# Pooled attention and a gated feed-forward on one core: next batch's loads, the order of the transpose queue, and when GpSimd pools

## The chip, the cores and the metric

One of the eight cores of a Trainium2 chip runs the kernel. The metric is the device time of one execution in microseconds (us), lower is better.

## The reference

Attention over pooled keys and values, then a feed-forward with the activation h * cos(h). Sizes: 8 batches, 8 heads, 576 rows, head size 64; keys and values are averaged over groups of 8 rows, which leaves 72. The feed-forward takes 4608 tokens of width 512 through 2048 and back.

```python
k_p = k.reshape(B, H, Sp, 8, D).mean(axis=3); v_p = the same of v
attn = softmax(q @ k_p.T / sqrt(D))
x = (attn @ v_p).transpose(0, 2, 1, 3).reshape(4608, 512)
h = x @ w_in
out = (h * cos(h)) @ w_out
```

## The kernel before

**Tiles.** The tokens are cut into nine tiles of 512 (loop `t`, line 550), the attention into eight batches of 576 rows. While tile t goes through the feed-forward, the attention of batch b = t + 1 is done between its matmuls, and the keys and values of batch b + 1 = t + 2 are loaded and pooled. The first batches and tile 0 have a path of their own; the change bears on tiles 1 to 7.

**Up phase** of a tile. Eight pairs of chunks of 128 columns (`up_mm`, line 336): TensorE multiplies w_in by xT into PSUM, ScalarE takes the cosine (line 352), VectorE multiplies both into `g_sb` (line 356). From tile 1 on, the output product is a fast scheme with seven smaller products instead of eight, for which VectorE forms the sums g1 to g4 of quarters of `g_sb` (`put_g`, line 381, both operands bf16 in SBUF). In steady tiles the first halves of g1 and g2 are formed after the fourth pair, of g3 after the fifth, of g4 after the sixth (line 570).

**Down phase.** The seven products (line 420) alternate between two banks, A and Bb; after each, VectorE reads the bank (`each`, lines 434 and 436; the `reads` list). In between TensorE does the attention of batch b: scores (line 222), whose exponentials ScalarE takes (line 229), and `values_rows` (line 276) for three chunks of 128 rows, later a fourth. `values_rows` ends with two VectorE operations (lines 287 and 289) that leave `x_rows`, and a DMA transpose on the sync queue that writes xT (line 293). The next tile's up phase needs xT.

**What sets the order.** There is no scheduler (`manual_schedule`): each engine and each queue runs in the order of the text. Three queues matter here.

- The sync queue (SP): four xT transposes of a tile, then its eight stores of 128 KB each (`rows_out`, line 451), issued in the last two reads (lines 446 and 447); then, in the next tile's up phase, the transpose of q (line 195, after the first pair) and of the pooled k (line 182, after the third), for the next batch.
- GpSimd: at the end of a tile's text a copy of one element of `kk` into `gate` (line 688). It makes GpSimd wait until the transpose of the pooled k has landed. Then GpSimd issues the loads of k, q and v of batch b + 1 (lines 114, 95, 114), and pools k and v in `pool_add` (lines 145 to 159): four steps from the staged tile into `half_sums` (line 151), two in `half_sums` (line 153), then two that write `kp2` for k, or one that writes `vz` for v. All are additions of 72 x 512 elements.
- VectorE: `g_sb` products, g sums, bank reads and the two operations of `values_rows`, in the order of the text.

The loads cast from fp32 to bf16 and move 576 KB each into SBUF. `kv_st` has two buffers, `qT` two, `o_two` two.

Of the kernel before, what the change touches and what calls it, by code (L numbers as in the profile page):

```python
# [12 lines left out]
ADD = mybir.AluOpType.add  # L13
# [7 lines left out]
def kernel(  # L21
# [9 lines left out]
    nc = tc.nc  # L31
    B, H, S, D = q.shape
# [37 lines left out]
    HF, HT, HM = FFCH // 2, TILE // 2, d_model // 2  # L70
    g1, g2, g3, g4 = [wpool.tile([128, HF, HT], BF16, name=f"g{i}") for i in range(1, 5)]
# [4 lines left out]
    kk = [wpool.tile([128, H, SpA], BF16, name=f"kk{i}") for i in range(2)]  # L76
# [9 lines left out]

    staged = {}

    def even_view(src, b, j0=0, j1=KCH):
        return src[b, 2 * j0:2 * j1].rearrange("(j a) (p t) d -> (a p) j (t d)", a=2, t=ROW)
# [18 lines left out]
    def load_kv(b, which, src):  # L111

        st = kv_tile()[:Sp, 0:H * POOL * D].rearrange("p (h t d) -> p h t d", h=H, t=POOL)
        nc.gpsimd.dma_start(out=st.rearrange("p h t d -> p h (t d)"),
                            in_=src[b].rearrange("h (p t) d -> p h (t d)", t=POOL))
        staged[which, b] = st

    def load_q(b):
        q_tile(b)
        load_even(staged["q", b], b, q)  # L120
# [21 lines left out]
            for r in range(2):  # L142
                copy(out=dst[half[r], pj0:pj1, a, 0:Sp], in_=ps[half[a]])

    def pool_add(b, which):

        st = staged.pop((which, b))
        x, s = st, half_sums
        add = nc.gpsimd.tensor_tensor
        for h in range(0, H, 2):  # L150
            add(out=s[:, h:h + 2], in0=x[:, h:h + 2, 0:4, :], in1=x[:, h:h + 2, 4:8, :], op=ADD)  # L151
        for h in range(0, H, 4):
            add(out=s[:, h:h + 4, 0:2, :], in0=s[:, h:h + 4, 0:2, :], in1=s[:, h:h + 4, 2:4, :], op=ADD)  # L153
        if which == "k":
            for slot in range(2):
                add(out=kp2[b % 2][:Sp, :, slot, :], in0=s[:, :, 0, :], in1=s[:, :, 1, :], op=ADD)  # L156
        else:
            s = s.rearrange("p (j a) t d -> p j a t d", a=2)
            add(out=v_part(b), in0=s[..., 0, :], in1=s[..., 1, :], op=ADD)
# [21 lines left out]
    def k_transpose(b):  # L181
        nc.sync.dma_start_transpose(out=kk[b % 2], in_=kp2[b % 2].rearrange("p h s d -> p (h s d)"))
# [198 lines left out]
    def put_g(k, i):  # L381
        f0, f1 = 4 * i, 4 * i + 4
        t1f1, t1f2, t2f1, t2f2 = [g_part(f, t, f0, f1) for t in range(2) for f in range(2)]
        out, x, y, op = {1: (g1, t2f1, t2f2, ADD), 2: (g2, g1[:, f0:f1], t1f1, SUB), 3: (g3, t1f1, t2f1, SUB),
                         4: (g4, t1f2, g2[:, f0:f1], SUB)}[k]
        nc.vector.tensor_tensor(out=out[:, f0:f1], in0=x, in1=y, op=op)  # L386
# [5 lines left out]
    def down_products(t):  # L392

        def of(w, m=0):
            return lambda fc: w[fc // 4][:, fc % 4, m * HM:(m + 1) * HM]

        def part(x):
            return lambda fc, p: x[:, fc, p * 128:(p + 1) * 128]

        apart = t == NT - 1  # L400
        if apart:
            A, Bb = [[x[:, 0:HM] for x in two] for two in (obanks, (banks[1][:, 0, :], banks[2][:, 0, :]))]
        else:
            A, Bb = [[obanks[i][:, p * HM:(p + 1) * HM] for p in range(2)] for i in (1, 0)]
        products = [
            (A, True, part(g_part(0, 0, 0, HF)), of(w_out_sb[0:2])),
            (Bb, True, part(g_part(1, 0, 0, HF)), of(w_out_sb[2:4])),
            (A, True, part(g2), of(w2)),
            (Bb, True, part(g1), of(w1)),
            (A, False, part(g3), of(w3)),  # L410
            (Bb, False, part(g4), of(w_out_sb[2:4], 1)),
            (A, False, part(g_part(1, 1, 0, HF)), of(w4)),
        ]
        mms = []
        for n, (bank, first, g, w) in enumerate(products):
            order = [(fc, p) for fc in range(HF) for p in range(2)]
            if apart and n == 6:
                order.sort(key=lambda x: x[1])
            for fc, p in order:
                mms.append(lambda bank=bank, first=first, g=g, w=w, fc=fc, p=p: nc.tensor.matmul(  # L420
                    bank[p], lhsT=g(fc, p), rhs=w(fc),
                    start=(first and fc == 0 and (apart or p == 0)), stop=(fc == HF - 1 and (apart or p == 1)),
                    skip_group_check=not first))

        p1, v16, q15 = [msb.tile([128, 2, HM], FP32, name=n, tag=n, bufs=1) for n in ("p1_sb", "v_sb", "q_sb")]
        o1, o2 = [msb.tile([128, 2, d_model], FP32, name="o_two", tag="o_two", bufs=2) for _ in range(2)]
        m1, m2 = slice(0, HM), slice(HM, d_model)

        def each(out, bank, other=None, m=slice(0, HM), tk=None):

            for p in range(2) if apart else (slice(0, 2),):
                ps = bank[p] if apart else obanks[1 if bank is A else 0].rearrange("p (a m) -> p a m", a=2)
                if other is None:
                    (nc.scalar.copy if t >= B - 1 else nc.vector.tensor_copy)(out=out[:, p, m], in_=ps)  # L434
                else:
                    nc.vector.tensor_tensor(out=out[:, p, m], in0=ps, in1=other[:, p], op=ADD)  # L436
                if apart and tk is not None:
                    rows_out(t, tk, out, (p,), m, (nc.sync, nc.scalar))

        reads = [  # L440
            lambda: each(p1, A),
            lambda: each(o1, Bb, p1, m1, 0),
            lambda: each(v16, A, p1),
            lambda: each(q15, Bb, p1),
            lambda: each(o2, A, q15, m2, 1),
            lambda: (each(o1, Bb, v16, m2, 0), apart or rows_out(t, 0, o1)),
            lambda: (each(o2, A, p1, m1, 1), apart or rows_out(t, 1, o2)),
        ]
        return [mms[i * 2 * HF:(i + 1) * 2 * HF] for i in range(7)], reads

    def rows_out(t, tk, o, ps=(0, 1), m=slice(0, d_model), queues=(nc.sync, nc.sync)):
        rows_of = out.rearrange("(b p t) m -> b t p m", b=B, t=ROW)
        for p in ps:
            for i, rows in enumerate(half):
                b_, pos = divmod((t * TILE + tk * HT + p * 128) // 64 + i, ROW)
                queues[i].dma_start(out=rows_of[b_, ORDER[pos], :, m], in_=o[rows, p, m])
# [36 lines left out]
    gate = consts.tile([1, 1], BF16, name="gate")  # L493
# [56 lines left out]
    for t in range(NT):  # L550
# [5 lines left out]
        for n, fp in enumerate(up_order(t)):  # L556
            up_mm(t, fp, 2 if n < 2 else 0)
            between = ()
            if t == 0:
                if fp == 4:  # L560
                    puts = pool_k_mm(1, obanks[0], 0, 2), pool_k_mm(1, obanks[1], 2, 4)
                elif fp in (5, 6):
                    g0 = 9 * (fp - 5)
                    puts = q_transpose_mm(1, obanks[0], g0, g0 + 5), q_transpose_mm(1, obanks[1], g0 + 5, g0 + 9)
                if fp in (4, 5, 6):
                    puts[0](vec)
                    between = ((puts[1], act),)
            up_g(t, fp, between)
            if 0 < t and 3 <= n < 6:
                put_gs(*[(k, 0) for k in (((3,), (1,), ()) if t == 1 else ((1, 2), (3,), (4,)))[n - 3]])  # L570
            if 0 < t and b < B:
                if n == 0:
                    q_transpose(b)
                elif n == 2:
                    k_transpose(b)
        mms = [(ms, fc) for ms in range(4) for fc in range(FFCH)]
        if t == 0:
            mms = [(ms, fc) for hm in range(2) for cg in (0, 2, 1, 3) for ms in range(2 * hm, 2 * hm + 2)
# [36 lines left out]
        else:  # L615
# [17 lines left out]
            def muls():  # L633
                while later:
                    later.pop(0)()
# [12 lines left out]
                put_g(2, 0)  # L648
            put_gs((1, 1), (2, 1))
            reads[0]()  # L650
            put_g(3, 1)
            reads[1]()
            if t == 1:
                put_g(4, 0)
            if steady:
                values_rows(*u0)
            product(2)
            reads[2]()
            muls()
            if steady:  # L660
                values_rows(*u1)
                values_rows(*u2)
# [20 lines left out]
            reads[6]()  # L683
        if t < B:
            sin_tables()
        if 0 < t and b + 1 < B:

            nc.gpsimd.tensor_copy(out=gate, in_=kk[b % 2][0:1, 0, 0:1])
        if b + 1 < B:
            load_kv(b + 1, "k", k)  # L690
            load_q(b + 1)
            load_kv(b + 1, "v", v)
            if t == 0:
                put_weights(0, nc.gpsimd, (3, 2, 4))
                put_weights(1, nc.gpsimd, (1,))
            pool_add(b + 1, "k")
            pool_add(b + 1, "v")
# [1 line left out]
_INS = ['q', 'k', 'v', 'moe_w_in', 'moe_w_out']  # L699
_OUTS = [((4608, 512), 'float32')]  # L700
# [25 lines left out]
```

The softmax here doesn't subtract the row's maximum and nothing guards it: scores larger than these inputs give would overflow.

## Time and profile before

| | us |
|---|---|
| median of 3 runs | 291.74 |
| lowest, highest | 290.35, 293.71 |
| span of the profiled run | 288.6 |
| first up matmul of tiles 2, 3, 4, 5, 6, 7, 8 | 84.09, 113.20, 143.89, 173.15, 202.56, 231.93, 258.57 |
| one step of pooling, line 151 / 153 / 156 (mean) | 1.195 / 1.305 / 1.329 |
| product into `g_sb`, line 356 (mean) | 1.221 |
| sum of two quarters of `g_sb`, line 386 (mean) | 0.760 |
| xT transpose, issue to landing (median, longest) | 5.8, 9.6 |
| load of k / q / v, issue to landing (median) | 7.7 / 10.2 / 14.4 |

How to read it: PE is TensorE, PEld its weight loads, DVE VectorE, ACT ScalarE, POOL GpSimd, SPq the sync queue. In a timeline each line has start, length, engine, line of the kernel, operation, output and input with their shapes, and in brackets how long the engine was idle just before and what ended that. A length includes time in which the operation stood at the head of its engine and could not go on.

### The profile page before, as it was taken

The numbers are of one execution on the slowest core, as the hardware profiler recorded it, in microseconds if no ns is written. First come the engines' busy times: TensorE is split into PE (matmuls) and PEld (weight loads), VectorE is DVE, ScalarE is ACT, GpSimd is POOL, SyncE is SP. The second block draws the span as 40 slices with busy tenths as digits, with TensorE's granted clock in tenths as the row PEclk, the third lists the DMA queues.
The fourth block names the chain that finished last, engine by engine and source line by source line (L and its number), as shares of the span: only waits on it lengthen the run. The fifth ranks groups of instructions, "written<-read, shape, count | busy, mean of one in ns | idle before, by whom it ended". The sixth has DMA issues, their size and how long they took to land.

```text
span 288.6 us, 5827 instructions
## 1 busy us (share of the span) xinstructions
PE 275.1 (95%) x2338; PEld 175.9 (61%) x2360; DVE 217.5 (75%) x314; ACT 164.2 (57%) x193; POOL 149.7 (52%) x145
## 2 busy tenths in 40 slices
PE   7889999999979999999799999999999999999994
PEld 2545554447854696468645884488448854884583
DVE  6458747799947995799549966996699669856972
ACT  3786798368147735773556655665557456436600
POOL 8563079996698359933995299529930000000000
PEclk9999999999999999999999999999999999999999
DMA  7999999554998699769977998699680243006014
GB/s 161 200 207 206 206 205 216 120 99 53 184 119 172 89 179 99 153 107 169 138 159 104 166 134 143 127 149 137 127 160 2 55 98 68 0 9 138 2 36 109
DMA packets 57545, 36.12 MB, mean 125 GB/s; under 512 B 35248, under 2 KB 53168, under 8 KB 57520
## 3 DMA queue, kind: packets, MB, share of 16 engines
q0 software_dynamic: 19744, 18.07, 39.9%
q1 hardware_dynamic: 37136, 17.18, 36.2%
q10 hardware_dynamic: 640, 0.52, 0.8%
q8 instruction: 18, 0.29, 0.4%
q14 instruction: 7, 0.06, 0.1%
HBM read 36.70 MB, written 9.44 MB: 160 GB/s over the span
## 4 chain that ended last, share of the span: by engine, by line
PE 61%; DVE 8%; DMA 3%; ACT 2%; issue 1%; DVEq 0%
PE obank L420 27%; PE bank L342 25%; DVE g_sb L356 4%; PE obank L342 3%; DMA xT<-x_rows 3%; PE bank L222 2%; DVE g L386 2%; PE bank L420 2%; PE bank L284 2%; ACT cos L352 1%; DVE o_two L436 1%; PE bank L257 1%; ACT ex L229 0%; DVE xT L268 0%; ACT inv L263 0%
## 5 line engine op out<-in xcount | busy, mean ns | idle before, releaser
L342 PE MATMUL bank<-xT,w_in_sb 128*128 128x512 bf16 x495 | 113.0, 379 | 4.1 <-DMA xT<-x_rows 1.6
L352 ACT ACTIVATE cos<-bank,half_pi 128x1024 f32<-128x1024 f32 x64 | 70.3, 1113 | 60.5 <-PE bank L342 59.9
L356 DVE TENSOR_TENSOR g_sb<-bank,cos 128x1024 bf16<-128x1024 f32 x64 | 77.1, 1221 | 29.2 <-ACT cos L352 29.2
L342 PEld LDWEIGHTS <-w_in_sb 128*128 128x128 bf16 x576 | 55.8, 98 | 70.1 <-DMA xT<-x_rows 3.6
L151 POOL TENSOR_TENSOR half_sums<-kv_st 72x512 f32<-72x512 bf16 x48 | 56.1, 1195 | 26.7 <-DMA kv_st<-in_k_dram 26.3
L229 ACT ACTIVATE ex<-bank 72x1024 bf16<-72x1024 f32 (+1 forms) x40 | 35.0, 928 | 34.5 <-PE bank L222 34.4
L420 PEld LDWEIGHTS <-g 128*128 128x128 bf16 x512 | 47.9, 98 | 6.1 <-issue 0.3
L420 PE MATMUL obank<-w,g 128*128 128x256 bf16 x368 | 42.6, 272 | 0.2 <-DVE p_sb L434 0.2
L420 PEld LDWEIGHTS <-g_sb 128*128 128x128 bf16 x384 | 36.6, 98 | 7.8 <-DVE g_sb L356 1.3
L153 POOL TENSOR_TENSOR half_sums<-half_sums 72x512 f32<-72x512 f32 x24 | 30.8, 1305 | 0.0
L420 PE MATMUL obank<-w_out_sb,g_sb 128*128 128x256 bf16 x240 | 29.2, 273 | 0.5 <-DVE g_sb L356 0.5
L386 DVE TENSOR_TENSOR g<-g_sb 128x1024 bf16<-128x1024 bf16 x32 | 24.3, 760 | 0.5
L289 DVE TENSOR_TENSOR x_rows<-bank,inv_rows 128x512 bf16<-128x512 f32 x24 | 16.6, 692 | 0.8
L268 DVE TENSOR_TENSOR xT<-bank,inv 64x256 bf16<-64x256 f32 x14 | 5.9, 422 | 14.6 <-ACT inv L264 14.6
L156 POOL TENSOR_TENSOR kp<-half_sums 72x512 bf16<-72x512 f32 x12 | 15.7, 1329 | 0.5
L420 PE MATMUL obank<-w_out_sb,g 128*128 128x256 bf16 x112 | 15.6, 273 | 0.0
L420 PE MATMUL obank<-w,g_sb 128*128 128x256 bf16 x128 | 15.3, 273 | 0.0
L342 PE MATMUL obank<-xT,w_in_sb 128*128 128x512 bf16 x64 | 15.1, 379 | 0.0
L359 PE MATMUL obank<-w_out_sb,g_sb 128*128 128x512 bf16 x61 | 14.7, 379 | 0.4 <-issue 0.3
L386 DVE TENSOR_TENSOR g<-g_sb,g 128x1024 bf16<-128x1024 bf16 x16 | 12.9, 809 | 0.0
L222 PE MATMUL bank<-qT,kk 64*72 64x128 bf16 (+2 forms) x288 | 12.5, 221 | 0.1
L320 ACT ACT_TABLE_LOAD x9 | 11.5, 1283 | 0.9 <-PEq L710 0.7
(102 smaller groups left out, 262.9 us busy)
## 6 DMA issues: line engine op xcount, KB each, us to landing
out_dram<-o_two SPq DMA_DIRECT2D x64, 128.0 KB, 2.4
kv_st<-in_v_dram POOLq DMA_DIRECT2D x8, 576.0 KB, 14.4
kv_st<-in_k_dram POOLq DMA_DIRECT2D x7, 576.0 KB, 7.7
q_b<-in_q_dram POOLq DMA_DIRECT2D x6, 576.0 KB, 10.2
w_in_sb<-in_moe_w_in_dram POOLq DMA_DIRECT2D x4, 512.0 KB, 13.5
w_out_sb<-in_moe_w_out_dram POOLq DMA_DIRECT2D x4, 512.0 KB, 18.3
q_b<-in_q_dram POOLq DMA_DIRECT2D x4, 288.0 KB, 12.4
g_sb<-in_k_dram SPq DMA_DIRECT2D x1, 576.0 KB, 3.5
```

Source lines behind the costliest of these rows:

```text
L151: add(out=s[:, h:h + 2], in0=x[:, h:h + 2, 0:4, :], in1=x[:, h:h + 2, 4:8, :], op=ADD)
L153: add(out=s[:, h:h + 4, 0:2, :], in0=s[:, h:h + 4, 0:2, :], in1=s[:, h:h + 4, 2:4, :], op=ADD)
L156: add(out=kp2[b % 2][:Sp, :, slot, :], in0=s[:, :, 0, :], in1=s[:, :, 1, :], op=ADD)
L222: nc.tensor.matmul(pair[:Sp, bank, c:c + n].rearrange("p (g n) -> p g n", n=64), lhsT=kk[b % 2][half[r], h0 + i, 0:Sp], rhs=att["qT", b][h ...
L229: nc.scalar.activation(out=ex[:, 0:nh * n].rearrange("p (a n) -> p a n", a=2), in_=pair[:Sp, :, 0:nh * n // 2], func=ACTF.Exp, scale=scale ...
L289: nc.vector.tensor_tensor(out=x[0:n].rearrange("p (j a d) -> p j a d", j=KCH, a=2), in0=ps[0:n, :, 0:2 * (D + 2)].rearrange("p j (a w) -> ...
L342: nc.tensor.matmul(h[j] if h is obanks else h[:, j, :], lhsT=w_in_sb[fc // 4][:, ki, (fc % 4) * 128:(fc % 4 + 1) * 128], rhs=xT[:, ki, t * ...
L352: nc.scalar.activation(out=c, in_=ps, func=ACTF.Sin, bias=half_pi[:, :1])
L356: nc.vector.tensor_mul(out=o, in0=ps, in1=c)
L359: nc.tensor.matmul(o, lhsT=g_sb[:, fc, ms * 128:(ms + 1) * 128], rhs=w_out_sb[fc // 4][:, fc % 4, :], start=(fc == 0), stop=(fc == FFCH - 1))
L386: nc.vector.tensor_tensor(out=out[:, f0:f1], in0=x, in1=y, op=op)
L420: mms.append(lambda bank=bank, first=first, g=g, w=w, fc=fc, p=p: nc.tensor.matmul(bank[p], lhsT=g(fc, p), rhs=w(fc), start=(first and fc ...
```

## The change

Four edits, all in the steady tiles. (1) The transposes of q and k go ahead of the stores of the tile before: the two last reads put their stores into a list, and the list is emptied after the transposes, in the next up phase. (2) The loads of batch b + 1 move from the end of the tile's text to the up phase, after the transpose of the pooled k: the gate on `kk` and k's load stand between v's first four steps of pooling and its last three, the loads of q and v behind these. (3) At the end of a tile, where GpSimd begins to pool the next batch, a new gate copies one element of g3: pooling starts after VectorE has formed the second half of g3. (4) `values_rows` of the first chunk stands ahead of that sum and of the read of bank Bb. The aims are loads that are over before the xT transposes start, transposes that don't stand behind stores, and fewer meetings of GpSimd's additions with VectorE's sums. The amount of work is the same on TensorE, VectorE and ScalarE; GpSimd has one more one-element copy per tile.

```diff
-    staged = {}
+    staged, stores = {}, []
@@
-    def pool_add(b, which):
-        st = staged.pop((which, b))
-        x, s = st, half_sums
-        add = nc.gpsimd.tensor_tensor
+    def pool_first(b, which):
+        x, s = staged.pop((which, b)), half_sums
         for h in range(0, H, 2):
-            add(out=s[:, h:h + 2], in0=x[:, h:h + 2, 0:4, :], in1=x[:, h:h + 2, 4:8, :], op=ADD)
+            nc.gpsimd.tensor_tensor(out=s[:, h:h + 2], in0=x[:, h:h + 2, 0:4, :], in1=x[:, h:h + 2, 4:8, :], op=ADD)
+
+    def pool_rest(b, which):
+        s, add = half_sums, nc.gpsimd.tensor_tensor
         for h in range(0, H, 4):
@@
-            lambda: (each(o1, Bb, v16, m2, 0), apart or rows_out(t, 0, o1)),
-            lambda: (each(o2, A, p1, m1, 1), apart or rows_out(t, 1, o2)),
+            lambda: (each(o1, Bb, v16, m2, 0), apart or stores.append(lambda: rows_out(t, 0, o1))),
+            lambda: (each(o2, A, p1, m1, 1), apart or stores.append(lambda: rows_out(t, 1, o2))),
@@
                 elif n == 2:
                     k_transpose(b)
+                    if b + 1 < B:
+                        nc.gpsimd.tensor_copy(out=gate, in_=kk[b % 2][0:1, 0, 0:1])
+                        load_kv(b + 1, "k", k)
+                    pool_rest(b, "v")
+                    if b + 1 < B:
+                        load_q(b + 1)
+                        load_kv(b + 1, "v", v)
+            if n == 2:
+                while stores:
+                    stores.pop(0)()
@@
             reads[0]()
+            if steady:
+                values_rows(*u0)
             put_g(3, 1)
             reads[1]()
             if t == 1:
                 put_g(4, 0)
-            if steady:
-                values_rows(*u0)
             product(2)
             reads[2]()
-            muls()
@@
-        if 0 < t and b + 1 < B:
-            nc.gpsimd.tensor_copy(out=gate, in_=kk[b % 2][0:1, 0, 0:1])
         if b + 1 < B:
-            load_kv(b + 1, "k", k)
-            load_q(b + 1)
-            load_kv(b + 1, "v", v)
             if t == 0:
+                load_kv(b + 1, "k", k)
+                load_q(b + 1)
+                load_kv(b + 1, "v", v)
                 put_weights(0, nc.gpsimd, (3, 2, 4))
                 put_weights(1, nc.gpsimd, (1,))
-            pool_add(b + 1, "k")
-            pool_add(b + 1, "v")
+            else:
+                nc.gpsimd.tensor_copy(out=gate, in_=g3[0:1, HF - 1, 0:1])
+            pool_first(b + 1, "k")
+            pool_rest(b + 1, "k")
+            pool_first(b + 1, "v")
```

The removed `muls()` after `reads[2]` had nothing to do at that place.

## The prediction

> **What bounds the kernel now.** I read four views: busy times, busy time by stage, waits, and the timelines of single engines around each wait. The page first:
>
> ```profile
> span 288.6 us, 5827 instructions
> PE 275.1 (95%) x2338; PEld 175.9 (61%) x2360; DVE 217.5 (75%) x314; ACT 164.2 (57%) x193; POOL 149.7 (52%) x145
> ```
>
> TensorE is busy 95%, so only its gaps can be won, and whatever makes a new gap is paid in full. I cut the trace at the first up matmul of each token tile (L342); I call that moment U. Columns: stretch, length, busy time of PE, PEld, DVE, ACT, POOL, clock, DMA.
>
> ```profile
> 84.09:113.20 29.11, 29.00 (x254) 19.32 (x257) 22.34 (x32) 17.04 (x19) 20.51 (x20) 1.00 0.92 142
> 113.20:143.89 30.69, 29.00 (x255) 19.33 (x257) 24.95 (x37) 17.04 (x19) 20.42 (x20) 1.00 0.95 135
> 143.89:173.15 29.26, 29.02 (x255) 19.23 (x258) 22.30 (x32) 17.04 (x19) 20.41 (x20) 1.00 0.95 141
> 173.15:202.56 29.41, 29.05 (x255) 19.32 (x258) 23.53 (x35) 17.04 (x19) 20.72 (x20) 1.00 0.98 140
> ```
>
> Tiles 2 to 5 each hold 29.0 us of matmuls and last 29.11, 30.69, 29.26 and 29.41. What lies above 29.1 is loss: 1.58 in tile 3, under 0.4 in the others. A further loss ends tile 1. The waits name them:
>
> ```profile
> PE bank L342 <- DMA xT<-x_rows: 1.6, 1, 1.6
> PE bank L342 <- DVE o_two L436: 1.5, 1, 1.5
> PEld L342 <- DMA xT<-x_rows: 3.6, 2, 1.9
> POOL gate L688 <- DMA kk<-kp: 14.2, 4, 4.7
> ```
>
> The 1.5 us at 84.09 is put down to VectorE, but the weight load there waits for the xT transpose too, so both large gaps (1.46 and 1.58) are late transposes. The first transpose before 143.89 was issued at 133.71, while the loads issued at 127.08 to 129.53 still ran; it landed 9.6 us later, after the last load, against 2.4 us at best for that line. The fourth line says why the loads are late: GpSimd waits for kk before it may load.
>
> **What the Trainium skill says.** "SBUF — State Buffer", section "SBUF: two separate sides": VectorE and GpSimd share a port pair as an exclusive lock; a VectorE operation with two SBUF inputs and a GpSimd operation that reads SBUF cannot run together, and the one that starts second waits for the whole of the other. The trace agrees, and shows that they take turns:
>
> ```profile
> 53.95 1.05 DVE L376 TENSOR_TENSOR w<-w,w_out_sb 128x1024 bf16<-128x1024 bf16 x1
> 55.04 1.64 DVE L376 TENSOR_TENSOR w<-w_out_sb,w 128x1024 bf16<-128x1024 bf16 x1
> 54.53 1.59 POOL L156 TENSOR_TENSOR kp<-half_sums 72x512 bf16<-72x512 f32 x1
> 181.48 1.26 POOL L159 TENSOR_TENSOR vz<-half_sums 72x512 bf16<-72x512 f32 x1
> 182.13 1.17 DVE L386 TENSOR_TENSOR g<-g_sb 128x1024 bf16<-128x1024 bf16 x1
> ```
>
> A sum of two bf16 tiles alone takes 0.69. At 182.13 it takes 1.17: it ends 0.6 after the pooling step ends at 182.74. At 53.95 the sum ran first, GpSimd's step took the lock at its end (hence 1.59 instead of 1.26), and the next sum waited for that whole step (1.64). Products that read PSUM (L356) keep their 1.22 beside any pooling.
>
> "DMA: Bandwidth & Descriptors", section "SWDGE vs HWDGE vs iDMA": software and hardware queues feed different internal queues, served in turn. Here a transpose beside loads does move, but lands only when they are done (the 9.6 us above).
>
> **What VectorE's slack is.** The up phase has four sums (g1, g2 after the third pair of products, g3, g4 later) between products. In tile 3, where nothing collides:
>
> ```profile
> 122.19 0.69 DVE L386 TENSOR_TENSOR g<-g_sb 128x1024 bf16<-128x1024 bf16 x1
> 122.91 0.69 DVE L386 TENSOR_TENSOR g<-g,g_sb 128x1024 bf16<-128x1024 bf16 x1
> 124.66 0.68 DVE L386 TENSOR_TENSOR g<-g_sb 128x1024 bf16<-128x1024 bf16 x1
> 188.68 0.83 PE L420 MATMUL obank<-w_out_sb,g_sb 128*128 128x256 bf16 x6 [0.25 <-DVE g_sb L356]
> ```
>
> The seventh product (a fourth of g_sb that the first down product needs) starts at 126.98 and is done 1.13 later, U+14.9. TensorE ends the up phase at U+13.8 and has 12 matmuls of 0.11 before it needs this piece: U+15.1. So the slack is 0.2 us. The last line, of tile 5, proves it: there the collision at 182.13 cost 0.5, the product ended at U+15.5 and TensorE waited; the tile took 0.3 longer than tile 2.
>
> **The change, part by part.**
>
> *Transposes ahead of stores.* Eight stores take 6.2 us of the sync queue (114.76 to 121.0) ahead of these:
>
> ```profile
> 121.11 2.89 SPq L195 DMA_TRANSPOSE qT<-q_b  x1
> 124.09 1.23 SPq L182 DMA_TRANSPOSE kk<-kp  x1
> 126.96 0.18 POOL L688 COPY gate<-kk 1x1 bf16<-1x1 bf16 x1 [4.72 <-DMA kk<-kp]
> ```
>
> Now q's starts when the last xT transpose is issued, U+1.5, and k's at U+1.6+2.9 = U+4.5; kp is ready by about U+1. GpSimd saw kk 2.87 after that issue (124.09 to 126.96), so the gate opens at U+7.35 instead of U+13.8. The stores follow at U+5.7 and are landed by about U+13; o_two is next written at about U+19, so they cost nothing.
>
> *Loads early.* k's load (0.85 of GpSimd's time) is issued at U+7.5, q's and v's after v's pooling, about U+13.2 to U+14.9, 1.3 to 2 us ahead of before in steady tiles. Three loads took 16.3 us (127.08 to 143.37); without k's share, which took 7.6, I estimate 9 to 10 from q's issue, done at U+24 of a tile of 29 to 30.6. The xT transposes then have 5 us left, and land on time. At tile 1's end q and v are issued no earlier (67.9), but k's load is gone by then: v lands near 79 instead of 82.9, ahead of 82.6. Won: 1.46 + 1.58, and 0.1 in tile 4.
>
> *values_rows ahead of g3.* The first transpose starts about 1 us earlier; g3 and the read of obank come 0.9 later, at 105.0 on tile 2's scale, just when TensorE wants that bank (105.06). Nothing either way.
>
> *Pooling held behind g3.* The gate opens at about U-8.7 of the next tile; k's pooling began at U-8.8 to U-9.3 before. Four of L151 (4.5), two of L153 (2.5), two of L156 (2.5) and four for v (4.5) end at about U+5.6, with one wait for g4's second half. Nothing, except that this sum, at about 107.8, is due on TensorE at 109.0: 0 to 0.6 per tile, by where it meets a step of 1.1 us. I take 0.
>
> *v's last three steps behind the gate.* This decides. Before, they ran at U+5.2 to U+9.3 and touched at most g1. Now, in tiles 2 to 5, they start at U+7.35+0.12+0.85 = U+8.3 (step 1.23, sum 0.60, product 1.13):
>
> ```
> step 1 8.3-9.5   g1 (ready 9.0) 9.5-10.1
> step 2 10.1-11.4 g2 (ready 10.2) 11.4-12.0
> step 3 12.0-13.2 product 12.0-13.1, g3 13.2-13.8
> product 13.8-14.9, g4 15.0-15.6, seventh product 15.6-16.7
> ```
>
> The piece comes at U+16.7 instead of U+15.1: TensorE waits 1.5 to 1.6 us per tile. Bounds: 0 if the three steps meet no sum, 1.9 if step 1 starts 0.3 later but still ahead of g1. I take 1.5. Tile 1 is spared (fewer sums), tile 6 too (no gate there). Behind the waiting sums stand the products, and behind these TensorE, which has nothing else to run.
>
> **Sum.** Won: 1.46 + 1.58 + 0.1 + 0.3 (tile 5's old collision) = 3.5. Lost: 4 x 1.5 = 6.0. Net +2.5: 291.7 + 2.5 = 294.2.
>
> **Rivals.**
> - *A: no collision counts.* The gate opens after U+9, so that g1 and g2 pass first, or VectorE gets the lock at once. For: 0.7 us later is enough. Against: the queue ahead of kk is only q's transpose, and turn-taking is seen at 53.95. Then 291.7 - 3.5 = 288.2.
> - *B: half of it.* One step's wait per tile (0.8, less the 0.2 of slack): 291.7 - 3.5 + 2.4 = 290.6. For: a gate near U+8.0 or U+8.9 shifts who goes first.
> - *C: more.* g4's second half also loses its turn, 0.6 in each of five tiles: 294.2 + 3.0 = 297.2. For: GpSimd's start is now tied to VectorE's g3, so the meeting repeats in every tile. Against: by my sums g4 comes 0.1 before a step ends.
>
> **How the numbers follow.** Forecast 0.45, A 0.2, B 0.2, C 0.15. The forecast's own spread is 292.5 to 295.8 (stall 1.1 to 1.9). The range 288.5 to 297.0 leaves out the better half of A and the worse part of C. Faster by over 1% (under 288.8): A, most of it, 0.18. Slower by over 1% (over 294.7): C and about 0.4 of the forecast, plus a little, 0.37. Within 1%: 0.45.
>
> **What would show it.** Right: gate near U+7.4; the sums g1 and g2 at 1.2 us instead of 0.69 in tiles 2 to 5; TensorE waiting for VectorE at the end of the up phase; these tiles 30.5 to 30.7 long; no wait for xT. Wrong: sums at 0.69 while the tiles last 29.1, or xT waits that stay.

## The result and the profile after

The changed kernel takes 305.78 us (median of 4 runs, 304.61 to 306.96), the kernel before 291.05 beside it (289.92 to 293.71). The ratio is 1.049, 95% interval 1.040 to 1.059: slower by 14.7 us. The forecast was 294.2 with a range to 297.0. It had the direction and the place of the loss, and a sixth of its size.

The page of the changed kernel: span, busy times and, in 40 slices, the granted clock of TensorE in tenths.

```profile
span 302.8 us, 5822 instructions
PE 281.5 (93%) x2338; PEld 178.2 (59%) x2360; DVE 230.4 (76%) x314; ACT 164.2 (54%) x193; POOL 152.3 (50%) x150
...
PEclk9999999999999799979999999979999999999999
```

The same 2338 matmuls keep TensorE busy 6.4 us longer, and VectorE, with the same 314 instructions, is busy 12.9 us longer. Three slices have a lower clock; before the change there was none. The stretches of tiles 2 to 5 (from first up matmul to first up matmul; columns as before: stretch, length, busy times of PE, PEld, DVE, ACT, POOL, clock, DMA):

```profile
83.42:117.30 33.88, 30.84 (x257) 19.93 (x256) 26.71 (x35) 17.03 (x19) 21.42 (x21) 0.95 0.68 122
117.30:150.58 33.28, 30.72 (x257) 20.04 (x257) 26.23 (x35) 17.04 (x19) 21.16 (x21) 0.95 0.69 124
150.58:182.88 32.30, 29.21 (x257) 19.34 (x256) 26.39 (x35) 17.04 (x19) 21.17 (x21) 1.00 0.72 128
182.88:216.40 33.52, 30.74 (x257) 19.87 (x256) 26.45 (x35) 17.04 (x19) 21.18 (x21) 0.95 0.68 123
98.55:102.12 3.57, 3.57 (x10) 1.35 (x10) 3.41 (x4) 1.11 (x1) 0.00 (x0) 0.52 1.12 213
```

The tiles last 32.3 to 33.9 instead of 29.1 to 30.7. Two effects make up the difference. First, length minus busy time is 2.6 to 3.1 us in each: TensorE waits. Second, three of the four are busy 1.5 to 1.6 longer than the other (tile 4), at a mean clock of 0.95. The last line shows where: directly behind tile 2's wait the clock is 0.52. The waits, and both kinds of stretch behind the gap:

```profile
PE bank L344 <- DVE g_sb L358: 10.6, 4, 2.9
POOL gate L580 <- DMA kk<-kp: 7.9, 4, 2.0
```

```profile
98.55 3.57 PE L344 MATMUL bank<-xT,w_in_sb 128*128 128x512 bf16 x8 [2.88 <-DVE g_sb L358]
...
165.48 1.89 PE L344 MATMUL bank<-xT,w_in_sb 128*128 128x512 bf16 x8 [2.66 <-DVE g_sb L358]
```

In each of tiles 2 to 5, TensorE waits before the eighth pair for a bank that VectorE's product must clear: 2.88, 2.40, 2.66 and 2.62. The same eight matmuls then take 1.89 at full clock and 3.57 at half. The waits for xT are gone from the list. What VectorE and GpSimd do before the first of these gaps (tile 2, U = 83.42):

```profile
92.40 3.29 DVE L388 TENSOR_TENSOR g<-g_sb 128x1024 bf16<-128x1024 bf16 x1
95.72 1.63 DVE L388 TENSOR_TENSOR g<-g,g_sb 128x1024 bf16<-128x1024 bf16 x1
```

```profile
91.65 0.18 POOL L580 COPY gate<-kk 1x1 bf16<-1x1 bf16 x1 [2.01 <-DMA kk<-kp]
91.77 0.85 POOL L114 DMA_DIRECT2D kv_st<-in_k_dram  x1
92.64 2.50 POOL L155 TENSOR_TENSOR half_sums<-half_sums 72x512 f32<-72x512 f32 x2
95.22 1.59 POOL L161 TENSOR_TENSOR vz<-half_sums 72x512 bf16<-72x512 f32 x1
```

g1 is ready at U+9.0, as forecast. It takes 3.29 where a free sum takes 0.69, because it waits for *both* steps of L155 (92.64 to 95.14). Only then is it let in; L161 follows it, and g2 waits for the whole of that (1.63). The forecast had g1 run between the two L155 steps.

**The account.** From the first up matmul of tile 1 to that of tile 7 the kernel takes 14.2 us more.

| term | us |
|---|---|
| four waits before the eighth pair | +10.6 |
| three stretches at half clock (3.41 us each, which costs 1.7) | +5.1 |
| a new wait in tile 1 | +0.7 |
| left over: +0.7 more busy time of TensorE that is not half clock, +0.1 in gaps under 0.3 | +0.8 |
| the two xT waits that went | -3.0 |
| sum | +14.2 |

The left-over busy time was not traced further: tile 4, which has no half clock, is busy 29.21 instead of 29.02. The ends of matmuls are modelled in the profile, and the excess can come from there.

### The profile page after: what moved, and what is told of

Same layout as the page of the kernel before. It is cut to its first block, busy times and chain, and to the rows that moved or that the text cites. A ratio compares the mean times of both kernels' runs of the same rounds, so it can differ in the third digit from the quotient of the medians.

```text
span 302.8 us, 5822 instructions
## 1 busy us (share of the span) xinstructions
PE 281.5 (93%) x2338; PEld 178.2 (59%) x2360; DVE 230.4 (76%) x314; ACT 164.2 (54%) x193; POOL 152.3 (50%) x150
## 4 chain that ended last, share of the span: by engine, by line
PE 68%; DVE 22%; ACT 4%; issue 2%; DMA 2%; POOL 0%; DVEq 0%; POOLq 0%; ACTq 0%
PE obank L422 27%; PE bank L344 27%; DVE g L388 10%; DVE g_sb L358 9%; PE obank L361 4%; ACT cos L354 3%; PE bank L224 3%; DMA q_b<-in_q_dram 2%; PE bank L422 2%; PE obank L344 2%; PE bank L259 1%; DVE o_two L438 1%; PE bank L286 1%; ACT ex L231 1%; DVE vz L180 0%
## 5 line engine op out<-in xcount | busy, mean ns | idle before, releaser
L344 PE MATMUL bank<-xT,w_in_sb 128*128 128x512 bf16 x495 | 117.9, 389 | 11.4 <-DVE g_sb L358 10.6
L344 PEld LDWEIGHTS <-w_in_sb 128*128 128x128 bf16 x576 | 56.9, 99 | 79.5 <-issue 16.4
L358 DVE TENSOR_TENSOR g_sb<-bank,cos 128x1024 bf16<-128x1024 f32 x64 | 77.0, 1219 | 28.2 <-ACT cos L354 28.1
L149 POOL TENSOR_TENSOR half_sums<-kv_st 72x512 f32<-72x512 bf16 x48 | 56.6, 1205 | 0.5
L422 PEld LDWEIGHTS <-g_sb 128*128 128x128 bf16 x384 | 37.3, 99 | 9.8 <-DVE g_sb L358 2.1
L388 DVE TENSOR_TENSOR g<-g_sb 128x1024 bf16<-128x1024 bf16 x32 | 34.1, 1067 | 0.5
L422 PE MATMUL obank<-w_out_sb,g_sb 128*128 128x256 bf16 x240 | 30.0, 277 | 1.3 <-DVE g_sb L358 1.3
L155 POOL TENSOR_TENSOR half_sums<-half_sums 72x512 f32<-72x512 f32 x24 | 30.4, 1286 | 0.1
L707 POOL COPY gate<-g 1x1 bf16<-1x1 bf16 x5 | 0.9, 179 | 44.1 <-DVE g L388 44.1
L270 DVE TENSOR_TENSOR xT<-bank,inv 64x256 bf16<-64x256 f32 x14 | 5.9, 422 | 14.3 <-ACT inv L266 14.2
L388 DVE TENSOR_TENSOR g<-g,g_sb 128x1024 bf16<-128x1024 bf16 x16 | 14.8, 927 | 0.5
L361 PE MATMUL obank<-w_out_sb,g_sb 128*128 128x512 bf16 x61 | 14.7, 379 | 0.4 <-issue 0.3
```

The costliest lines, as they stand in the source:

```text
L149: nc.gpsimd.tensor_tensor(out=s[:, h:h + 2], in0=x[:, h:h + 2, 0:4, :], in1=x[:, h:h + 2, 4:8, :], op=ADD)
L344: nc.tensor.matmul(h[j] if h is obanks else h[:, j, :], lhsT=w_in_sb[fc // 4][:, ki, (fc % 4) * 128:(fc % 4 + 1) * 128], rhs=xT[:, ki, t * ...
L358: nc.vector.tensor_mul(out=o, in0=ps, in1=c)
L361: nc.tensor.matmul(o, lhsT=g_sb[:, fc, ms * 128:(ms + 1) * 128], rhs=w_out_sb[fc // 4][:, fc % 4, :], start=(fc == 0), stop=(fc == FFCH - 1))
```

## The experiments

Two theories to begin with. **L**: the loss is the port between GpSimd and VectorE; v's last three steps, behind the gate and the load, meet g1 and g2 and hold them longer than by turns. **D**: the early loads themselves cost the time. A third question is the half clock: cause of its own, or a consequence of the gaps? All ratios are against the kernel before, run on the same chip beside.

| kernel | median us | ratio (95%) |
|---|---|---|
| changed kernel | 305.78 | 1.049 (1.040 to 1.059) |
| v's steps ahead of the gate | 298.29 | 1.026 (1.020 to 1.032) |
| TensorE kept busy in the gaps | 300.35 | 1.031 (1.026 to 1.036) |
| k's load behind v's steps | 293.85 | 1.008 (1.004 to 1.012) |
| one step fewer behind the gate | 295.44 | 1.016 (1.011 to 1.021) |
| half-size steps | 295.09 | 1.015 (1.009 to 1.021) |
| v's steps ahead, steps chained | 294.51 | 1.011 (1.008 to 1.014) |
| changed kernel, steps chained | 295.08 | 1.015 (1.013 to 1.018) |
| v's steps ahead, first values back | 290.77 | 1.000 (0.998 to 1.001) |
| no hold behind g3 | 312.09 | 1.071 (1.065 to 1.077) |
| before + values of chunk 0 first | 292.46 | 1.005 (1.002 to 1.007) |
| before + early transposes | 287.71 | 0.989 (0.986 to 0.991) |
| the same + early loads in tile 1 | 287.04 | 0.988 (0.986 to 0.991) |

### v's steps ahead of the gate

```diff
                     k_transpose(b)
+                    pool_rest(b, "v")
                     if b + 1 < B:
                         nc.gpsimd.tensor_copy(out=gate, in_=kk[b % 2][0:1, 0, 0:1])
                         load_kv(b + 1, "k", k)
-                    pool_rest(b, "v")
```

> The changed kernel, with v's last three pooling steps ahead of the gate on kk instead of behind it; all else stays (loads early, transposes first, gate on g3, first chunk ahead of g3). Theory L (the three steps hold the port that g1 and g2 need; the gap this makes on TensorE then costs a window at half clock): the steps end near U+9.3, as before the change, g1 waits at most 0.7 us, tiles 2 to 5 last 29.1 to 29.5 us, the clock stays at 1.0, xT is never waited for: 288 to 291 us. Rival D (the early loads, which now run beside the stores, or the new gate on g3, or the first chunk's earlier place, slow the tiles): those are all still there, so the time stays at 300 us or more.

Measured: 298.29, between the two. g1 and g2 take 0.69 in every tile and the waits before the eighth pair are gone. That part of L holds, and the loads, which stay early in tiles 2 to 5, do no harm to the up phase. In place of the old wait stands another one. The waits, then VectorE and GpSimd in tile 2's down phase:

```profile
PE obank L422 <- DVE g L388: 7.0, 4, 1.8
PE bank L344 <- DMA xT<-x_rows: 1.8, 1, 1.8
```

```profile
107.83 4.37 DVE L388 TENSOR_TENSOR g<-g_sb,g 128x1024 bf16<-128x1024 bf16 x1
```

```profile
104.57 0.18 POOL L707 COPY gate<-g 1x1 bf16<-1x1 bf16 x1 [9.44 <-DVE g L388]
104.71 4.48 POOL L149 TENSOR_TENSOR half_sums<-kv_st 72x512 f32<-72x512 bf16 x4
109.16 2.48 POOL L155 TENSOR_TENSOR half_sums<-half_sums 72x512 f32<-72x512 f32 x2
111.72 2.83 POOL L158 TENSOR_TENSOR kp<-half_sums 72x512 bf16<-72x512 f32 x2
```

g4's second half arrives in the third of six steps and gets in only after the sixth: 4.37 us, in all four tiles (4.36 to 4.38). In the changed kernel the same sum takes 0.75 each time. It arrives there 0.95 us into a step, here 0.88. The mechanism that the forecast called rival C exists, but in this kernel, not in the changed one. So a sum can be held over several steps. Two questions follow: where is it let in, and what does the half clock cost?

### TensorE kept busy in the gaps

Twelve matmuls whose result nobody reads go ahead of the eighth pair in tiles 2 to 5; the work of the kernel is complete.

```diff
+            if 1 < t < B - 2 and n == 7:
+                for i in range(12):
+                    nc.tensor.matmul(obanks[1], lhsT=w_in_sb[0][:, 0, 0:128], rhs=w_in_sb[0][:, 1, :])
```

> The changed kernel, with 12 matmuls of 128x512 whose result nobody reads, put in tiles 2 to 5 ahead of the eighth pair of the up phase, where TensorE waits 2.4 to 2.9 us for the product that frees its bank. They take 12 x 0.216 = 2.6 us and lie in the wait. Theory L says that the gap, not the work, brings the half clock: with the gap filled the clock stays at 1.0, and each of the three or four tiles that lost a window of 3.41 us at half speed wins back 1.7 us: 299 to 301 us, tiles of 31.9 to 32.4. Rival H (the slow clock has another cause, and would come anyway): 306 us or more, clock near 0.98, as the matmuls then only add.

Measured: 300.35 (300.20 without the one run at 305.07), 5.4 less than the changed kernel, although TensorE has more to do. The profile is of the run at 305.07; its clock was at half from 14.46 to 24.70, ahead of tile 1, and full from there on, so the gaps of tiles 2 to 5 can be read in it. The gap of tile 3:

```profile
132.99 2.75 PE L561 MATMUL obank<-w_in_sb 128*128 128x512 bf16 x12
135.60 1.89 PE L344 MATMUL bank<-xT,w_in_sb 128*128 128x512 bf16 x8
```

VectorE's sums are as late as ever (g1 2.86, g2 1.64 in this tile), but the eighth pair runs at full clock in all four. So the half clock is a consequence of the gap and not of the loads or the sums, and it is worth 5.4 us of the 14.7, a little more than the 5.1 of the account. (The account is of a run with three such stretches. Two of the four runs of the changed kernel are 2.3 us longer at a mean clock of 0.978 instead of 0.983; a fourth stretch would give that clock, and 1.7 of the 2.3.)

### When the steps start, and how many stand behind the gate

Two edits of the changed kernel, told together. In the first, k's load goes behind v's three steps, which then start 0.85 earlier. In the second, one of the two L155 steps goes to the end of v's first part, so that two steps stay behind gate and load.

```diff
                         nc.gpsimd.tensor_copy(out=gate, in_=kk[b % 2][0:1, 0, 0:1])
-                        load_kv(b + 1, "k", k)
                     pool_rest(b, "v")
                     if b + 1 < B:
+                        load_kv(b + 1, "k", k)
```

> The changed kernel, with k's load issued behind v's last three steps instead of ahead of them; the gate stays ahead of both. The steps then start 0.85 us earlier, at about U+8.1 instead of U+9.0. Theory L with two steps that are not parted: g1, ready at U+9.0, waits until the second step ends, U+10.6, so 1.6 us instead of 2.5 to 2.7; the gap on TensorE falls to 1.5 to 1.8 us and the half clock comes in fewer tiles or in none: 294 to 300 us. Rival I (it is the issue of the load on GpSimd that holds VectorE off, not the steps): the first sum then waits 0 to 1.2 us and the time falls to 290 to 293.

```diff
-        for h in range(0, H, 4):
+        for h in range(0 if which == "k" else 4, H, 4):
...
             pool_first(b + 1, "v")
+            nc.gpsimd.tensor_tensor(out=half_sums[:, 0:4, 0:2, :], in0=half_sums[:, 0:4, 0:2, :],
+                                    in1=half_sums[:, 0:4, 2:4, :], op=ADD)
```

> The changed kernel, with the first of v's two steps in half_sums ahead of the gate, so that one of them and the step into vz stand behind it. Theory L: g1 waits for one step instead of two, about 1.3 us (U+9.0 to U+10.3), g2 for the last one, about 1.0; the gap on TensorE is 1.2 to 1.6 us instead of 2.4 to 2.9, which is too short for the half clock: tiles of 30.4 to 30.8 us, 293 to 296 us, the sum that the forecast had. Rival: a wait of any length over 1 us brings the half clock: 298 to 302.

Measured: 293.85 and 295.44. With the earlier start the four gaps are under 0.2, 1.49, 0.29 and 0.45; g1 takes 1.27, 1.89, 0.70, 0.86. In tile 3 g1 arrives 1.16 us into the first L155 step and is shut out for the second, in tile 4 it arrives 1.12 us into it and is let in between: two arrivals 0.04 us apart, and a sum that takes 1.2 us more in one of them. The wait for xT at the end of tile 1 is back, 2.12. The time lies just under the range of L and above that of rival I (the issue of the load holds VectorE off), and g1's waits would fit I too. What speaks against I is the first experiment: with v's steps ahead of the gate the sums run freely beside the issues (last section).

With one step fewer the gaps are 1.80, 1.43, 1.24 and 1.67, g1 2.20 at most, and no stretch at half clock follows. That is what the forecast had taken for the changed kernel, 1.5 per tile, and its time is within 1.3 us of the forecast's 294.2. One more step without a hand-over made the gap 1.1 longer (mean 2.64 against 1.54), and with it came the half clock.

### Half-size steps

```diff
-        for h in range(0, H, 4):
-            add(out=s[:, h:h + 4, 0:2, :], in0=s[:, h:h + 4, 0:2, :], in1=s[:, h:h + 4, 2:4, :], op=ADD)
+        for h in range(0, H, 2):
+            add(out=s[:, h:h + 2, 0:2, :], in0=s[:, h:h + 2, 0:2, :], in1=s[:, h:h + 2, 2:4, :], op=ADD)
```

> The changed kernel with each of the two middle pooling steps cut into two of half the size; nothing else moves. The four wait for nothing between them. Theory L (no sure hand-over between steps that wait for nothing): g1 is still held for all that is left of the four, 2.5 to 3.4 us, gap 2.2 to 2.9 per tile, 303 to 308 us. Rival S (a sum waits for the one step that runs, so its length is the cost): g1 takes 1.3 at most, gap about 1.2, no half clock, 293 to 297 us.

Measured: 295.09, the time of rival S. The trace says something else. VectorE and GpSimd in tile 4 (the second GpSimd line shows the last of the four steps by itself), and then in tile 3:

```profile
152.89 2.51 DVE L388 TENSOR_TENSOR g<-g_sb 128x1024 bf16<-128x1024 bf16 x1
...
122.66 0.69 DVE L388 TENSOR_TENSOR g<-g_sb 128x1024 bf16<-128x1024 bf16 x1
123.39 1.10 DVE L388 TENSOR_TENSOR g<-g,g_sb 128x1024 bf16<-128x1024 bf16 x1
```

```profile
152.74 3.24 POOL L155 TENSOR_TENSOR half_sums<-half_sums 72x256 f32<-72x256 f32 x4
154.79 1.18 POOL L155 TENSOR_TENSOR half_sums<-half_sums 72x256 f32<-72x256 f32 x1
...
122.82 4.07 POOL L155 TENSOR_TENSOR half_sums<-half_sums 72x256 f32<-72x256 f32 x4
```

In tiles 4 and 5 g1 comes 0.15 after the first step has begun. It waits for three of the four (2.51 and 2.50) and goes in ahead of the last, which takes 1.18 instead of 0.72 because it waits for g1. So the sum gets its turn neither after one step, as S had it, nor only when the row is over, as L had it; the gaps there are 1.56 and 1.55, and L had expected 2.2 at least. In tiles 2 and 3 g1 comes 0.16 to 0.24 before the first step and goes first; a gap of 1.01 before a down product is left. The total falls into the range of S by this mixture. By the trace neither S nor L holds as it stood.

### Steps chained

From the kernel with v's steps ahead of the gate: the middle step, in halves, directly behind the step whose output it reads, so that every second step must wait for the one before.

```diff
         for h in range(0, H, 2):
             add(out=s[:, h:h + 2], in0=x[:, h:h + 2, 0:4, :], in1=x[:, h:h + 2, 4:8, :], op=ADD)
+            add(out=s[:, h:h + 2, 0:2, :], in0=s[:, h:h + 2, 0:2, :], in1=s[:, h:h + 2, 2:4, :], op=ADD)
...
-        for h in range(0, H, 4):
-            add(out=s[:, h:h + 4, 0:2, :], in0=s[:, h:h + 4, 0:2, :], in1=s[:, h:h + 4, 2:4, :], op=ADD)
```

> From the kernel with v's last three steps ahead of the gate (298.3): the steps of half the size stand each directly behind the step whose output they read, so that every second step of GpSimd waits for the one before it. Same sums, four steps more. Theory L (GpSimd keeps the port from step to step while the next step waits for nothing, and a waiting sum gets it for certain only at a step that waits for its forerunner): g4's second half waits for at most one pair of steps, takes at most 2.6 us instead of 4.37, TensorE's four gaps of 1.75 before the next product shrink below 0.6, 289 to 293 us. Rival W (a waiting sum is let in only when GpSimd runs out of work): g4's half still waits for all of k's pooling, 4 us or more, 297 to 301 us.

Measured: 294.51 (292.2 to 295.3). The time misses what L expected by 1.5, the lines don't. g4's second half and the steps around it, in tile 2:

```profile
110.06 0.68 DVE L387 TENSOR_TENSOR g<-g_sb,g 128x1024 bf16<-128x1024 bf16 x1
```

```profile
108.86 1.15 POOL L149 TENSOR_TENSOR half_sums<-kv_st 72x512 f32<-72x512 bf16 x1
110.09 1.24 POOL L150 TENSOR_TENSOR half_sums<-half_sums 72x256 f32<-72x256 f32 x1
111.29 1.15 POOL L149 TENSOR_TENSOR half_sums<-kv_st 72x512 f32<-72x512 bf16 x1
```

The sum slips into the 0.08 us between L149's end and the dependent step, and it is that step that waits (1.24 instead of 0.72). g4's half takes 0.68 in every steady tile instead of 4.37, the gaps of 1.75 are gone and tiles 2 to 5 last 29.98, 29.53, 29.71 and 29.39 instead of 31.1 to 32.7. What costs time in the profiled run, at 292.20 the shortest of the ten, is the end of tile 1: there v's pooling and with it the loads come later, and TensorE waits 3.15 us for xT (1.77 in the kernel it was made from). The other runs, longer by 0.3 to 3.1, were not profiled; eight of them had a mean clock of 0.988 to 0.994 instead of 0.998, so part of it is half clock.

### The changed kernel with its steps chained

The same edit on the changed kernel itself. Now only L160, v's last step, stands behind gate and k's load.

> The changed kernel, with gate, loads and holds all as they are; only the pooling steps are cut and ordered so that each half-size step follows the step whose output it reads, and only v's last step stands behind the gate and k's load. Theory L: g1 meets that single step at worst and takes 1.9 at most, g2 0.7, the gap before the eighth pair is under 0.7, no half clock, 288 to 293 us. Rival (the early loads or the gate cost time by themselves, whatever stands behind them): gaps of over 1.5 stay in tiles 2 to 5, 297 us or more.

Measured: 295.08, 10.7 us better than the changed kernel, with gate, loads and holds where they were, but not the 288 to 293. Before the eighth pair no gap is left in tiles 3 to 5 (0.92 in tile 2). One step is left behind the load, and it meets a later sum, here in tile 3:

```profile
127.91 1.62 DVE L387 TENSOR_TENSOR g<-g_sb 128x1024 bf16<-128x1024 bf16 x1
```

```profile
132.45 0.83 PE L421 MATMUL obank<-w_out_sb,g_sb 128*128 128x256 bf16 x6 [1.22 <-DVE g_sb L357]
```

g3's first half waits for that single step, the seventh product comes later, and TensorE stands 1.22 us, in each of tiles 3 to 5. This is the wait that the forecast had named (the piece for the first down product), from one step. Tile 1 has again an xT wait, 1.81.

### First values back behind g3

From the kernel with v's steps ahead of the gate: `values_rows(*u0)` goes back to its old place, behind g3 and the read.

```diff
             reads[0]()
-            if steady:
-                values_rows(*u0)
             put_g(3, 1)
             reads[1]()
...
+            if steady:
+                values_rows(*u0)
             product(2)
```

> From the kernel with v's last three steps ahead of the gate (298.3): the values of the first chunk go back behind the third sum g3. That sum then ends 0.9 us earlier, and GpSimd's steps, held behind it, start 0.9 us earlier, while g4's second half keeps its place. Theory L (whether a waiting sum is let in between two steps that do not wait depends on where in the step it arrives): g4's half meets another place in the row of steps, takes at most 1.8 instead of 4.37, the gaps of 1.75 go, 288 to 291 us. Rival (the hold behind g3 puts the row of steps over g4's half wherever it starts): it still takes 3 us or more and the gaps stay above 1, 295 us or more.

Measured: 290.77, the time of L, and not by L's lines: the sum was to take 1.8 at most. VectorE and TensorE in tile 2:

```profile
107.17 3.41 DVE L388 TENSOR_TENSOR g<-g_sb,g 128x1024 bf16<-128x1024 bf16 x1
```

```profile
110.63 0.61 PE L422 MATMUL obank<-w_out_sb,g 128*128 128x256 bf16 x4 [0.63 <-DVE g L388]
```

g4's half arrives 0.74 us into the fourth step and still waits through both L155 steps. But the row of steps, tied to g3, begins 1.3 us earlier in the tile (at U+19.2 instead of U+20.5), and so does the hand-over at its end: the sum ends at U+26.8 instead of U+28.1, and of the gap of 1.74 only 0.63 is left. Here the place of the row, not the number of turns, decided. The whole set of edits, in an order that keeps the row's end early enough, costs nothing against the kernel before, and wins nothing.

### No hold behind g3

The changed kernel without its third edit; k's pooling starts when its load has landed.

```diff
-            else:
-                nc.gpsimd.tensor_copy(out=gate, in_=g3[0:1, HF - 1, 0:1])
```

> The changed kernel without one part, the hold of k's pooling behind VectorE's sum g3; GpSimd starts on k as soon as its load has landed, near U+15. If the loss is v's three steps behind the gate alone: g1 is held as before, gaps of 2.4 to 2.9 in tiles 2 to 5 with the half clock behind most, 303 to 308 us. Rival (the hold sets the phase in which g1 meets the steps, or keeps the sums g1 to g4 of the down phase free): g1 changes in each tile and the time moves by more than 3 us, up or down.

Measured: 312.09, 6.3 more. g1 takes 3.69, 2.91, 3.13 and 2.92, so the old loss stays, and the sums of the down phase now meet k's pooling, in tile 2:

```profile
106.54 1.14 DVE L388 TENSOR_TENSOR g<-g_sb 128x1024 bf16<-128x1024 bf16 x1
107.71 1.53 DVE L388 TENSOR_TENSOR g<-g,g_sb 128x1024 bf16<-128x1024 bf16 x1
...
110.60 1.54 DVE L388 TENSOR_TENSOR g<-g_sb 128x1024 bf16<-128x1024 bf16 x1
```

In the changed kernel the hold is worth 6.3 us. Of the rival's two halves the second is borne out, that the hold keeps the sums of the down phase free; g1 itself moved by 0.4 us in tile 2 and by 0.1 in the others. The hold isn't needed everywhere: the kernel with the early transposes alone, below, has early loads and no hold, and is faster than the one before.

### Single parts on the kernel before

**The values of chunk 0 ahead of g3**, the fourth edit alone:

> The kernel before with one part of the change alone: the values of the first chunk ahead of the third sum g3. The forecast: nothing either way, 290.5 to 291.5 us. From the profile of the changed kernel: the read of the bank comes late for the fourth product, 0.2 us in each of tiles 1 to 6, 291.8 to 292.6 us; and if k's pooling, which is not tied to g3 here, meets g4's second half otherwise than before, up to 1.2 per tile more.

Measured: 292.46, 1.5 us more. The forecast's "nothing either way" was wrong by that much. The profile, of a run at 294.75, doesn't settle where it goes: there are gaps of 0.47, 0.20 and 0.28 before a down product in tiles 2, 5 and 6, and xT is waited for three times (1.72, 0.72 and 2.17, ahead of tiles 2, 4 and 5), the last time with a stretch of half clock behind it.

**The transposes ahead of the stores**, the first edit alone (the list of stores, emptied after the transposes; loads, holds and pooling as before):

> The kernel before with one part of the change alone: q's and k's transposes ahead of the stores. The gate stays behind v's pooling, which stays at U+5 to U+9; it opens near U+9.4 instead of U+13.8, and the three loads follow at once. Theory L (nothing but sums that meet steps without waits cost time): both waits for xT go, 3.0 us won, v's steps stay clear of g1 and g2 and k's pooling comes 4 us earlier: 287.5 to 289.5 us, if that pooling meets no sum; with one sum per tile caught for 1.2 to 1.8, 292 to 298. Rival (the early transposes themselves cost time on the sync queue or at the stores): no gap before a product, yet 291 or more, with a wait for a store or for q's transpose.

Measured: 287.71, 1.1% faster than before. The gate stands behind v's last step here and cannot collide with g1: it opens at U+7.7 in tile 3 (124.25), and the three loads are out by U+10.3 instead of U+16.3 before. Tiles 3 to 6 last 28.95 each. What is left, in the profiled run, is at tile 1's end, where xT is 2.16 late and a stretch of half clock follows, and in tile 2, where a down product waits 0.83 behind sums that met k's pooling.

**That, and the early loads in tile 1 only**, where fewer sums stand in the way:

```diff
                     k_transpose(b)
+                    if t == 1:
+                        nc.gpsimd.tensor_copy(out=gate, in_=kk[b % 2][0:1, 0, 0:1])
+                        load_kv(b + 1, "k", k)
+                        pool_rest(b, "v")
+                        load_q(b + 1)
+                        load_kv(b + 1, "v", v)
...
+            if t == 1:
+                nc.gpsimd.tensor_copy(out=gate, in_=g3[0:1, HF - 1, 0:1])
```

> The kernel with the early transposes alone (287.7), and in tile 1 only also the early loads of the change, k's ahead of v's last three steps, with k's pooling of that tile behind g3; the transposes for tile 2 came 2.16 us late in the former, and a window at half clock followed (1.75). If these two are what is left: tile 1 at about 30.3 instead of 31.7, tile 2 at 29.0 to 29.8 instead of 31.6, 283.5 to 285.5 us. Rival (the sums of tile 1 lose as much at v's steps, or the loads land no earlier): 287 us or more.

Measured: 287.04 (286.77 to 287.70), 1.2% faster than before (interval 0.9 to 1.5%) and the fastest of all. Tiles 1, 2 and 5:

```profile
53.14:83.43 30.29, 29.30 (x258) 19.33 (x256) 28.04 (x36) 17.03 (x19) 25.89 (x24) 1.00 0.68 116
83.43:112.38 28.95, 28.95 (x259) 19.36 (x257) 23.25 (x35) 17.03 (x19) 21.65 (x20) 1.00 0.88 143
...
170.27:199.22 28.95, 28.95 (x259) 19.40 (x257) 23.62 (x35) 17.04 (x19) 21.59 (x20) 1.00 0.84 143
```

The tiles came as expected, 30.29 and 28.95: from tile 2 on TensorE is busy 28.95 of 28.95 us. The time did not come down to 285.5, because it was worked out from the profiled run of the kernel with the early transposes alone, at 290.9 the longest of its 20; the others lie at 286.7 to 289.8. Against their median the gain is 0.7 and not sure.

## Why the prediction was wrong, point by point

- **Transposes ahead of stores, the gate at U+7.35.** It opened at U+8.2, 7.8, 8.0 and 8.0. The xT transpose ahead of them took longer to issue than the 1.2 us taken:

```profile
83.86 2.01 SPq L295 DMA_TRANSPOSE xT<-x_rows  x1
86.04 2.69 SPq L197 DMA_TRANSPOSE qT<-q_b  x1
88.81 1.25 SPq L184 DMA_TRANSPOSE kk<-kp  x1
```

  q's issue starts at U+2.6 instead of U+1.5, k's at U+5.4 instead of U+4.5. An error of 0.4 to 0.9: the steps meet g1 at another moment than in the schedule.
- **Won, 1.46 + 1.58.** Right, and by the way foreseen: v's load of tile 1 landed at 78.88 ("near 79"), and no wait for xT is left in tiles 1 to 5. The early transposes alone win 3.3.
- **Values ahead of g3, "nothing either way".** Wrong by a little: alone it costs 1.5. In the changed kernel little of that can be seen: all gaps under 0.3 together grew by 0.15.
- **Pooling behind g3, "I take 0".** Right for the changed kernel: g4's second half takes 0.75. Rival C, which had it lose its turn, did not come there; the run with v's steps ahead of the gate shows how near it was.
- **v's last three steps, "they take turns": the step that failed.** The schedule gave each sum the port after one step. It was read from one place, the sums at 53.95 and 55.04, and from the skill's lock. "SBUF — State Buffer", section "SBUF: two separate sides", says that whoever starts first holds the pair for the whole instruction; on who is next when both wait, the forecast had only that place. There the first sum is let in ahead of a step that must wait for its forerunner (L156 after L153), the second between two that need not wait. The profile before holds more of the second kind, which the forecast did not use: at 77.49, 107.50, 136.68, 167.31 and 196.86 a sum met GpSimd's steps in the down phase and was let in after one of them. So turns were all that this profile could show; they did not carry over to v's steps behind the load. Between the two L155 steps g1 was not let in, in 4 tiles of 4. g1 took 3.29, 2.81, 3.07 and 3.03 instead of 1.2, and the stall was 2.4 to 2.9 instead of 1.5. The upper bound of 1.9 rested on the same turns, so the range was too narrow as well. That steps that must wait for their forerunner let the sum in is shown by the two chained kernels; that it was the number of steps in the row, by the kernel with one fewer.
- **A term that the sum did not have: the clock.** 4 x 1.5 would have stayed at full clock, as the gaps of 1.24 to 1.80 with one step fewer did. The longer gaps brought the half clock, 5.4 us by the run with TensorE kept busy. A page of the skill, "TensorE: Matmul & The Clock Gate", section "Part 1: The HAM clock gate", says that the clock falls back to half after an idle window of some 3.4 us. No single gap here was that long; what these runs show in its place is below.

- **Small misreadings.** The first up matmul of tiles 6, 7 and 8 before the change starts at 202.40, 231.77 and 258.41 in the trace, 0.16 ahead of the times in the table; tile 5 then took 29.25, 0.14 more than tile 2 and not 0.3. The transpose issued at 133.71 landed at 143.25, just ahead of v's load (143.37), not behind it. The four gains add up to 3.44. Together they move the forecast by 0.2.

So the sum should have read: won 3.0; lost 10.6 at the sums, 5.1 to the clock, 0.7 in tile 1 and 0.8 that is left over. Tile 1 was taken as "spared"; its sum at 64.28 took 2.58, through both L155 steps like the others.

## What to carry to other kernels

When GpSimd's additions can meet VectorE's sums, don't count on turns: bound the wait by the whole row of steps that follow one another without waiting, even if a sum is often let in earlier, and either move the row out of the way or order it so that each step needs the one before. Where a gap in TensorE comes to 2 us, count the slower clock behind it as part of its price. Of a change made of several parts, try each alone: here the order of the transposes alone brought a gain, and v's steps behind the gate and the early load nearly all of the loss.

## What the runs showed of the hardware

- **Where a waiting sum is let in.** Between a step and one that must wait for it (a pause of 0.07 to 0.09 us in GpSimd's row) every sum seen was let in. Between two that need not wait, some were let in and some not, and how far into a step the sum came doesn't tell them apart. L149 to L149, a step of 1.15: 0.95 into it, yes (all four tiles of the changed kernel); 0.88, no (four of four with v's steps ahead); 0.31, yes (tile 1 of the changed kernel). From the fourth L149 step to L155: 0.74 to 0.76, no (four of four with the first values back); 0.71, yes (tile 1 of the changed kernel). L155 to L155 in v's pooling, a step of 1.26: from 0.24 before the step's start to 0.48 into it, no (five of five in the changed kernel); 0.96 and 1.12, yes; 1.16, no. The same two steps in k's pooling: 0.05 and 0.44, yes (the kernel with early loads in tile 1). Even ahead of a row it isn't sure: 0.24 before the first step behind a load's issue g1 was shut out in the changed kernel, and went first with half-size steps. The rule behind this wasn't found.
- **GpSimd's issues of loads held no sum back where no step followed.** With v's steps ahead of the gate, g1 (93.04) and g2 (93.77) take 0.69 each while k's and q's loads are being issued.
- **The half clock goes by windows on a fixed grid.** The trace's record of the granted clock changes on a grid of 3.413 us that runs through the kernel, and the skill's section named above says the same of the window (3413 ns, free-running). I added up TensorE's idle time in each such window of the profiled runs, from tile 1 on and without the last 12 us. Behind all 8 windows with 2.1 us or more of idle time the next window ran at half clock. Of the 12 with 1.5 to 2.05 us only one was followed by it (1.74). That fits tile 4 of the changed kernel, which was spared with a gap of 2.66: the grid cuts it at 163.4, and 2.05 of it fell into one window. Where the page speaks of an idle window, the measurement decides: some 60% of one was enough.
